# A tile of its own for the larger part of batch 0's queries

## The chip, the cores and the metric

The kernel runs on one core of a Trainium2 chip. The metric is the device time of one execution in microseconds. TensorE (PE) multiplies matrices, VectorE (DVE), ScalarE (ACT) and GpSimd (POOL) do the rest, and SyncE (SP) stores the output. Loads and stores are DMAs, which an engine issues and which then run by themselves.

## The reference

Two layers, one behind the other, on 8 batches of 576 tokens. The first is an attention with a compressed memory of 32 rows per head, the second a channel mixing.

```python
# attention: q, k, v (8, 8, 576, 64), phi (8, 8, 576, 32)
a = softmax(phi, axis=memory)
k_m, v_m = a^T k, a^T v                       # (batch, head, 32, 64)
x = softmax(q k_m^T / sqrt(64)) v_m           # heads side by side: (8, 576, 512)
# mixing: w_k (512, 1024), w_v (1024, 512), w_r (512, 512)
x_prev = x shifted by one token, zero in front
xk, xr = mu_k x + (1 - mu_k) x_prev, mu_r x + (1 - mu_r) x_prev
out = sigmoid(xr w_r) * (relu(xk w_k) ** 2 w_v)
```

All inputs and the output are float32; the kernel computes in bf16 between them.

## The kernel before

A token's number in its batch is 9 p + j, with p from 0 to 63 on the partitions (two heads fill 128) and j from 0 to 8 along the row. The tiles of one batch therefore have 128 rows, four groups of heads and nine tokens each. `qs` are two query tiles, one for even and one for odd batches, `kvs` and `ems` the same for keys with values and for the exponentials of phi.

Nothing is ordered by a scheduler. `PLAN` is a list of words that stand in the order in which the steps are written to the engines. `0:qu` is step `qu` of batch 0, `c0:0b` is a block of the product with w_k, `g:` and `o:` are blocks of the products with w_r and w_v, and `p:` is a load. Each engine takes its own steps in this order. A step that needs another engine's result waits for it, and everything behind it on that engine waits too. These waits are put in when the program is built, from what the steps read and write in which tile.

Most loads are issued by GpSimd, since they turn float32 into bf16 on the way. So its queue is a list of loads: a load that waits holds up all later ones. The words in `PRE` come first, then those of the plan:

```python
PRE = "q:0u id:"
# p:v:0g p:v:0h p:q:0t p:wk:0-4 p:wk:4-8 p:phi:1 p:k:1 p:q:1 p:wr:0-4 p:wv:0-2 p:v:1 p:wv:2-4 ...
PARTS = (slice(0, 3), slice(3, NJ))
```

Batch 0 is split finer than the others. Its phi and its keys are loaded by ScalarE's queue as float32 (`ph`, `k0f`) and cast by ScalarE and VectorE. Its queries come in two parts by j: `q:0u` loads j 3 to 8 and `q:0t` loads j 0 to 2, both into `qs[0]` (line 186). `turn_part` (line 375) transposes one part for the scores: word `0:qu` the larger part, word `0:qt` the smaller one. In the plan `0:qu` stands ahead of `p:q:0t`. The other batches' queries go through `turn_q` (line 367).

In the names of the profile, `kvps` is the product of the exponentials with keys or values (line 285), `scps` the scores (line 392 for the parts, line 413 for whole batches), `pk`, `pr` and `pv` the products with w_k, w_r and w_v (lines 636, 669, 686), and `idle` are filler matmuls on zeros (line 225) with which the plan fills stretches in which TensorE has nothing to do. `rl` and `sq` are the relu and its square (lines 644 and 651), `x` the attention's output (line 477), `qT` the transposed queries.

The pool `work` has a ring of three places under the tag `x`. Batch 0's two halves of `k0f` take the first two; the attention outputs `x` of batches 1 to 7 follow.

Of the kernel before, what the change touches and what calls it, by code (L numbers as in the profile page):

```python
# [11 lines left out]
BF16 = mybir.dt.bfloat16  # L12
# [58 lines left out]
NJ = 9  # L71
# [5 lines left out]
def kernel(  # L77
# [13 lines left out]
    nc = tc.nc  # L91
    B, H, S, D = q.shape
# [12 lines left out]
    PARTS = (slice(0, 3), slice(3, NJ))  # L105
# [7 lines left out]
    work = ctx.enter_context(tc.sbuf_pool(name="work", bufs=2))  # L113
# [8 lines left out]
    HH = H // 2  # L122
    ROWS = (slice(0, 64), slice(64, 128))
    kvs = [const.tile([128, 2, HH, NJ, D], BF16, name=f"kv{i}") for i in range(2)]
    qs = [const.tile([128, HH * NJ, D], BF16, name=f"q{i}") for i in range(2)]
# [7 lines left out]
    def rows(src):  # L133
        return src.rearrange("h s d -> (h s) d").rearrange("(a p j) d -> p a (j d)", a=HH, j=NJ)

    def load_phi(b, eng):
        ph = ld.tile([128, HH, NJ, M], F32, name="ph", tag="ph")
        eng.dma_start(out=ph.rearrange("p h j m -> p h (j m)"), in_=rows(phi[b]))  # L138
        loads[b] = ph

    def load_rows(dst, src):
        nc.gpsimd.dma_start(out=dst.rearrange("p h j d -> p h (j d)"), in_=rows(src))  # L142

    def load_parity(dst, src, r):
        nc.gpsimd.dma_start(out=dst[r].rearrange("p h j d -> p h (j d)"), in_=rows(src)[r])
# [3 lines left out]
    for gs in (slice(0, 2), slice(2, 4)):  # L149
        k0.append(work.tile([128, 2, NJ, D], F32, name="k0f", tag="x", bufs=3))  # L150
        nc.scalar.dma_start(out=k0[-1].rearrange("p h j d -> p h (j d)"), in_=rows(k[0])[:, gs])
    nc.vector.memset(zeros, 0.0)  # L152
    mu2 = const.tile([2 * ND, 128], F32, name="mu2")
    nc.sync.dma_start(out=mu2[:ND, :], in_=moe_mu_k.rearrange("(a b) -> a b", b=128))
# [12 lines left out]
    def preload(word):  # L167

        what, _, part = word.partition(":")
        if what in weights:  # L170
            dst, src = weights[what]
            f0, f1 = (int(x) * 128 for x in part.split("-"))
            nc.gpsimd.dma_start(out=dst[:, :, f0:f1], in_=src[:, :, f0:f1])  # L173
        elif what == "id":
            make_identity(nc, identity)
        else:
            n = int(part[0])
            if what == "phi":
                load_phi(n, nc.gpsimd)
            else:  # L180
                dst = qs[n % 2].rearrange("p (h j) d -> p h j d", j=NJ) if what == "q" else kvs[n % 2][:, "kv".index(what)]
                src = {"q": q, "k": k, "v": v}[what][n]
                if part[1:] in ("t", "u"):
                    js = PARTS["tu".index(part[1])]
                    cols = slice(js.start * D, js.stop * D)
                    nc.gpsimd.dma_start(out=dst[:, :, js].rearrange("p h j d -> p h (j d)"), in_=rows(src)[:, :, cols])
                elif part[1:] in ("g", "h"):
                    gs = slice(0, 2) if part[1] == "g" else slice(2, 4)
                    nc.gpsimd.dma_start(out=dst[:, gs].rearrange("p h j d -> p h (j d)"), in_=rows(src)[:, gs])
                elif part[1:]:  # L190
                    load_parity(dst, src, ROWS["ab".index(part[1])])
                else:
                    load_rows(dst, src)

    for word in PRE.split():
        preload(word)
# [50 lines left out]
    def attention(b):  # L247
# [112 lines left out]
        def q_tile():  # L360
            if "qT" not in st:
                st["qT"] = work.tile([128, HH, NJ * PB, 2], BF16, name="qT", tag="qT", bufs=2)
            return st["qT"]
# [9 lines left out]
        def turn_part(js):  # L373

            def go():
                dst = q_tile()[:, :, js.start * PB:js.stop * PB].rearrange("p g n h -> p g (n h)")
                src = qs[b % 2].rearrange("p (g j) d -> p g (j d)", j=NJ)[:, :, js.start * D:js.stop * D]
                nc.vector.transpose(dst.bitcast(U32), src.bitcast(U32))
            return go

# [326 lines left out]
    for n, word in enumerate(" ".join(PLAN).split()):  # L707
        who, _, name = word.partition(":")
        if who == "p":
            todo.append((n, -2, word, lambda name=name: preload(name)))  # L710
        elif who in mixes:
            todo.append((n, -1, word, mixes[who][name]))
        else:
            todo.append((n, int(who), word, attend[int(who)](name)))
# [36 lines left out]
```

## Time and profile before

| | us |
|---|---|
| median of 3 runs | 204.7 |
| lowest and highest of these | 204.52, 205.77 |
| the profiled execution | 205.92 |
| its span, first to last instruction | 204.1 |
| VectorE busy in it | 150.8 |
| ScalarE busy in it | 136.7 |
| mean clock granted to TensorE | 0.988 of full |

A row of the timeline has the start in us, the length in us, the engine, the line, the operation, the tiles (out <- in) and how many instructions were merged. In brackets stands the idle time of the engine just before, and what ended it. `DMA q<-in_q_dram` there means that the wait ended when that load landed, `issue` that the profile shows no cause. The largest groups of loads by issue, with the KB of one and the median time from issue to landing:

```profile
ph<-in_phi_dram POOLq DMA_DIRECT2D x7, 576.0 KB, 15.0
kv<-in_k_dram POOLq DMA_DIRECT2D x7, 576.0 KB, 15.8
q<-in_q_dram POOLq DMA_DIRECT2D x7, 576.0 KB, 18.6
kv<-in_v_dram POOLq DMA_DIRECT2D x7, 576.0 KB, 19.0
```

KB are those of the destination in bf16 for keys, values and queries; the source has twice as many.

### The profile page before, as it was taken

Reading aid. Unit: us, or ns where it says so; the run is one execution under the profiler, and the core shown is the slowest. Engines: PE = TensorE matmul, PEld = TensorE weight load, DVE = VectorE, ACT = ScalarE, POOL = GpSimd, SP = SyncE. Lnnn points to the kernel's source line nnn. Section 1 sums busy time; section 2 is a strip of 40 time slices with the busy share of each in tenths; the row PEclk is TensorE's granted clock in tenths of the full one; section 3 lists DMA queues with packets and bytes.
Section 4 is the critical chain, followed back from the end, with each engine's and each line's share of the span. In section 5 each row is a group of like instructions: output and inputs, shape, how many; then the busy total and the mean of one; then the engine's idle time right before and its main releaser. Section 6 shows DMA issues by size and latency. Waiting matters only on the chain.

```text
span 204.1 us, 5433 instructions
## 1 busy us (share of the span) xinstructions
PE 194.3 (95%) x2228; PEld 101.4 (50%) x2228; DVE 150.8 (74%) x318; ACT 136.7 (67%) x310; POOL 28.7 (14%) x43
## 2 busy tenths in 40 slices
PE   8898999999998999999998999999999999999992
PEld 8453665674444444544445864444444444444441
DVE  2266678798998998999996997999999655320351
ACT  2538699767869999899858697894638940646220
POOL 5077222211004400082000000000000000000000
PEclk9999999999999999999998899999999999999998
DMA  6999999999999999899999240042330133310085
GB/s 203 270 139 236 235 204 206 261 226 227 287 230 291 209 241 260 176 151 200 320 252 236 37 94 12 3 102 52 75 85 0 27 84 88 71 43 0 20 248 143
DMA packets 25033, 31.88 MB, mean 156 GB/s; under 512 B 2472, under 2 KB 19632, under 8 KB 25008
## 3 DMA queue, kind: packets, MB, share of 16 engines
q0 software_dynamic: 17360, 20.32, 53.5%
q1 hardware_dynamic: 6176, 8.92, 17.1%
q10 hardware_dynamic: 1472, 2.29, 3.3%
q8 instruction: 17, 0.28, 0.5%
q14 instruction: 8, 0.07, 0.1%
HBM read 38.28 MB, written 9.44 MB: 234 GB/s over the span
## 4 chain that ended last, share of the span: by engine, by line
PE 70%; DMA 19%; POOL 3%; ACT 3%; issue 1%; DVE 1%; DVEq 0%; POOLq 0%
PE pv L686 27%; PE pk L636 24%; PE pr L669 13%; DMA wr<-in_moe_w_r_dram 8%; DMA ph<-in_phi_dram 7%; DMA q<-in_q_dram 4%; PE kvps L285 3%; ACT x L477 2%; PE nops L342 1%; ACT em L261 1%; POOL kv L142 1%; PE scps L413 1%; POOL wk L173 1%; POOL ph L138 1%; PE zps L295 1%
## 5 line engine op out<-in xcount | busy, mean ns | idle before, releaser
L636 PE MATMUL pk<-xkT,wk 128*128 128x512 bf16 (+4 forms) x352 | 68.3, 342 | 0.0
L686 PE MATMUL pv<-wv,sq 128*128 128x512 bf16 (+3 forms) x328 | 66.7, 353 | 0.0
L644 ACT ACTIVATE rl<-pk 128x512 bf16<-128x512 f32 (+3 forms) x66 | 35.5, 556 | 22.5 <-PE pk L636 21.2
L636 PEld LDWEIGHTS <-wk 128*128 128x128 bf16 x352 | 33.1, 99 | 27.9 <-issue 1.8
L686 PEld LDWEIGHTS <-sq 128*128 128x128 bf16 x328 | 30.9, 98 | 29.3 <-issue 0.2
L692 DVE SCALAR_TENSOR_TENSOR o<-sg,pv 128x512 f32<-128x512 f32 (+3 forms) x41 | 24.4, 613 | 20.7 <-PE pv L686 16.8
L669 PE MATMUL pr<-wr,xrT 128*128 128x512 bf16 x144 | 35.1, 380 | 0.2 <-DMA wr<-in_moe_w_r_dram 0.2
L651 ACT ACTIVATE sq<-rl 128x512 bf16<-128x512 bf16 (+5 forms) x59 | 27.0, 494 | 0.9
L673 ACT ACTIVATE sg<-pr 128x512 f32<-128x512 f32 x36 | 20.7, 604 | 8.9 <-DVE o L692 6.2
L669 PEld LDWEIGHTS <-xrT 128*128 128x128 bf16 x144 | 13.6, 98 | 16.5 <-DMA wr<-in_moe_w_r_dram 0.4
L477 ACT CAST x<-nops 128x320 bf16<-128x320 f32 (+1 forms) x50 | 16.3, 417 | 7.6 <-PE nops L342 7.6
L653 DVE TENSOR_TENSOR sq<-rl 128x512 bf16<-128x512 bf16 (+5 forms) x45 | 14.2, 338 | 5.7 <-ACT rl L644 5.1
L502 DVE TENSOR_SCALAR mu_d<-diff,mu 128x576 bf16<-128x576 bf16 x42 | 13.8, 377 | 0.3
L225 PE MATMUL idle<-zeros 128*128 128x64 bf16 (+2 forms) x107 | 11.3, 275 | 2.0 <-DVE zeros L152 1.0
L261 ACT ACTIVATE em<-ph 128x1152 bf16<-128x1152 f32 (+1 forms) x9 | 9.4, 1063 | 5.7 <-DMA ph<-in_phi_dram 5.7
L463 DVE TENSOR_TENSOR atn<-e,lz 128x576 bf16<-128x576 bf16 (+2 forms) x18 | 11.7, 686 | 0.2
L489 DVE TENSOR_TENSOR diff<-x 128x1280 bf16<-128x1280 bf16 (+2 forms) x21 | 10.4, 552 | 1.1 <-ACT x L477 0.9
L370 DVE STREAM_TRANSPOSE qT<-q 128x576 uint32<-128x576 uint32 x14 | 10.4, 760 | 0.8 <-DMA q<-in_q_dram 0.7
L642 DVE TENSOR_SCALAR rl<-pk 128x512 bf16<-128x512 f32 (+3 forms) x14 | 8.4, 603 | 3.3 <-PE pk L636 2.5
L504 DVE TENSOR_TENSOR xkT<-x,mu_d 128x1152 bf16<-128x1152 bf16 x14 | 10.5, 754 | 0.3
L504 DVE TENSOR_TENSOR xrT<-x,mu_d 128x1152 bf16<-128x1152 bf16 x14 | 10.3, 750 | 0.1
L500 ACT ACTIVATE mu_d<-diff,mu 128x576 bf16<-128x576 bf16 x14 | 10.1, 794 | 0.4 <-DVE diff L490 0.4
(72 smaller groups left out, 154.8 us busy)
## 6 DMA issues: line engine op xcount, KB each, us to landing
out_dram<-o SPq DMA_DIRECT2D x59, 128.0 KB, 2.4
ph<-in_phi_dram POOLq DMA_DIRECT2D x7, 576.0 KB, 15.0
kv<-in_k_dram POOLq DMA_DIRECT2D x7, 576.0 KB, 15.8
q<-in_q_dram POOLq DMA_DIRECT2D x7, 576.0 KB, 18.6
kv<-in_v_dram POOLq DMA_DIRECT2D x7, 576.0 KB, 19.0
k0f<-in_k_dram ACTq DMA_DIRECT2D x2, 576.0 KB, 6.6
wk<-in_moe_w_k_dram POOLq DMA_DIRECT2D x2, 512.0 KB, 7.5
wv<-in_moe_w_v_dram POOLq DMA_DIRECT2D x2, 512.0 KB, 18.5
```

The costliest lines, as they stand in the source:

```text
L463: nc.vector.tensor_mul(st["at"][:, c, sl], st["e"][:, c, sl], st["lz"][:, c, sl])
L477: (nc.vector.tensor_copy if both and i > 1 else nc.scalar.copy)(st["x"][:, i, sl], pss[i])
L502: nc.vector.tensor_scalar_mul(t[:, i], st["d"][:, pr + i, :], mu1[:, o:o + 1])
L504: nc.vector.tensor_add(dst, st["x"][:, pr:pr + n], t)
L636: nc.tensor.matmul(pk[:, p0 - lo:p1 - lo], lhsT=wk_sb[:, di, fi * 128:(fi + 1) * 128], rhs=xk_T[:, di, p0 % RING:p0 % RING + p1 - p0], sta ...
L644: nc.scalar.activation(rl, pk, AF.Relu, scale=HALF ** 0.5)
L651: nc.scalar.activation(sq[:, fi, p:p + p1 - p0], rl[:, part], AF.Square)
L653: nc.vector.tensor_mul(sq[:, fi, p:p + p1 - p0], rl[:, part], rl[:, part])
L669: nc.tensor.matmul(pr, lhsT=xr_T[:, di, c0:c0 + 128], rhs=wr_sb[:, di, :], start=(di == 0), stop=(di == ND - 1))
L673: nc.scalar.activation(gated[t], pr, AF.Tanh, scale=0.5)
L686: nc.tensor.matmul(pv[:, cols], lhsT=sq[:, fi, p:p + 128], rhs=wv_sb[:, fi, cols], start=(fi == 0), stop=(fi == NF - 1))
L692: nc.vector.scalar_tensor_tensor(o[:, cols], in0=gated[t][:, cols], scalar=1.0, in1=pv[:, cols], op0=AL.add, op1=AL.mult)
```

## The change

The larger part of batch 0's queries gets a tile `q0u` of its own, of 128 rows x 4 groups x 6 tokens x 64 in bf16, which takes the third place of the ring under the tag `x`. The smaller part stays where it was in `qs[0]`. `q0` is the pair of both places; the load and `turn_part` take their place from it. The plan, `PRE` and the banks stay as they were, and so does the order of the instructions on every engine. In the built program GpSimd's load `q:0t` has lost its wait for VectorE; twelve loads later, the load of batch 2's keys names VectorE (besides ScalarE) among those whose reading of batch 0's keys it waits for.

```diff
+    js = PARTS[1]
+    q0 = (qs[0].rearrange("p (h j) d -> p h j d", j=NJ)[:, :, PARTS[0]],
+          work.tile([128, HH, js.stop - js.start, D], BF16, name="q0u", tag="x", bufs=3))
     nc.vector.memset(zeros, 0.0)
...
                 if part[1:] in ("t", "u"):
                     js = PARTS["tu".index(part[1])]
                     cols = slice(js.start * D, js.stop * D)
-                    nc.gpsimd.dma_start(out=dst[:, :, js].rearrange("p h j d -> p h (j d)"), in_=rows(src)[:, :, cols])
+                    dst = q0["tu".index(part[1])]
+                    nc.gpsimd.dma_start(out=dst.rearrange("p h j d -> p h (j d)"), in_=rows(src)[:, :, cols])
...
             def go():
                 dst = q_tile()[:, :, js.start * PB:js.stop * PB].rearrange("p g n h -> p g (n h)")
-                src = qs[b % 2].rearrange("p (g j) d -> p g (j d)", j=NJ)[:, :, js.start * D:js.stop * D]
+                src = q0[PARTS.index(js)].rearrange("p g j d -> p g (j d)")
                 nc.vector.transpose(dst.bitcast(U32), src.bitcast(U32))
```

## The prediction

> **What bounds the kernel now.** I read the page first, then the chain of waits, then the waits of TensorE and of the load queue, then the early stretch microsecond by microsecond.
>
> ```profile
> span 204.1 us, 5433 instructions
> ...
> PE 194.3 (95%) x2228; PEld 101.4 (50%) x2228; DVE 150.8 (74%) x318; ACT 136.7 (67%) x310; POOL 28.7 (14%) x43
> ...
> DMA  6999999999999999899999240042330133310085
> ```
>
> TensorE is busy for 194.3 of 204.1 us, so everything that can be gained by waiting less is in the other 9.8 us. The transfers run nearly full until about 112 us (slices of 5.1 us; a 9 is 90% or more). The chain of waits has the queue that the change touches at its start:
>
> ```profile
> 1.25 8.87 DMA q<-in_q_dram
> 10.12 0.02 issue
> 10.14 0.99 DVE qT L378
> 11.13 0.29 issue
> 11.42 0.76 POOL q L186
> ...
> 15.84 15.41 DMA wr<-in_moe_w_r_dram
> ```
>
> The larger part of the queries lands at 10.12, VectorE transposes it until 11.13, and only then GpSimd issues the smaller part and, behind it, every later load. The chain reaches TensorE when wr lands at 31.25. What those 30 us are worth is not their length but what TensorE waited for meanwhile. This is the view of waits between 19 and 60 us (in total, times, longest):
>
> ```profile
> PE idle L225 <- issue: 1.0, 1, 1.0
> PE scps L413 <- DVE qT L370: 0.4, 1, 0.4
> PE nops L342 <- DVE o L692: 0.2, 1, 0.2
> PE pr L669 <- DMA wr<-in_moe_w_r_dram: 0.2, 1, 0.2
> PE kvps L285 <- DMA kv<-in_k_dram: 0.2, 1, 0.2
> ```
>
> Loads end the last two directly, and the 0.4 through the transpose of batch 1's queries. The other two have other releasers.
>
> **Part 1, the wait that goes.** The queue's timeline:
>
> ```profile
> 2.63 1.43 POOL L189 DMA_DIRECT2D kv<-in_v_dram  x2
> 11.42 0.76 POOL L186 DMA_DIRECT2D q<-in_q_dram  x1 [7.36 <-DVE qT L378]
> 12.17 1.49 POOL L173 DMA_DIRECT2D wk<-in_moe_w_k_dram  x2
> 13.63 0.78 POOL L138 DMA_DIRECT2D ph<-in_phi_dram  x1
> 14.38 0.78 POOL L142 DMA_DIRECT2D kv<-in_k_dram  x1
> ```
>
> The smaller part is written into columns that the transpose doesn't read, but into the same tile, and so the built program made the load wait for the transpose: 7.36 us. With two tiles that wait is not in the built program any more. GpSimd then goes on at 4.06: 0.76 for the smaller part, 1.49 for the two of wk, 0.78 and 0.78 for phi and k of batch 1, until 7.9. The next, q of batch 1, waits in both built programs for the landing eight loads earlier, here the larger query part at 10.12. No instruction is added on any engine, and the new tile takes the third place of a three-place ring whose next user, x of batch 3, comes tens of us later. Cost 0; if that place were still held the wait would be seen on ScalarE's x casts.
>
> **Part 2, what the transfers gain.** Engine shares and GB/s by stretch (the last two numbers):
>
> ```profile
> 10.00:11.00 1.00, 1.00 (x7) 0.39 (x4) 0.86 (x1) 0.06 (x1) 0.00 (x0) 1.00 1.22 213
> 11.00:12.00 1.00, 1.00 (x41) 0.73 (x40) 0.37 (x2) 0.00 (x0) 0.58 (x1) 1.00 0.96 159
> 12.00:13.00 1.00, 0.90 (x41) 0.57 (x40) 0.62 (x4) 0.00 (x0) 1.00 (x3) 1.00 0.33 35
> 13.00:14.00 1.00, 1.00 (x52) 0.36 (x44) 0.69 (x3) 0.39 (x2) 1.00 (x2) 1.00 0.99 89
> 14.00:15.00 1.00, 1.00 (x40) 0.59 (x40) 0.48 (x1) 0.90 (x4) 1.00 (x2) 1.00 1.44 190
> ```
>
> GpSimd waits 7.36 us, but the transfers starve for much less, because what it had issued lasts until nearly 12. Against 213 the four stretches from 11 to 15 miss 54 + 178 + 124 + 23 = 379 KB, or 379 / 213 = 1.8 us. I take 1.8 for every landing behind it. The bounds are 0.8 (only the empty stretch 12 to 13 counts, 178 / 213) and 2.0 (a little for 15 to 16 beside). The loads ahead of the gap (larger query part, v, k) stand first in their queues as before: 0 for them, and VectorE has 0.63 us of idle behind the first transpose to cover a later landing:
>
> ```profile
> 11.75 0.61 DVE L323 TENSOR_SCALAR kbd<-kvps,rz 128x128 bf16<-128x128 f32 x2 [0.63 <-PE kvps L285]
> ...
> 15.13 0.58 DVE L378 STREAM_TRANSPOSE qT<-q 128x384 uint32<-128x384 uint32 x1 [0.16 <-DMA q<-in_q_dram]
> ```
>
> The second row is the smaller part's own transpose. It waited 0.16 us for its load; that goes, and is worth 0, because TensorE's wait at 18.82 (part 4) stands between it and the end.
>
> **Part 3, what TensorE gains.** The three waits in their places:
>
> ```profile
> 24.17 0.37 PE L295 MATMUL zps<-ones,em 128*128 128x2 bf16 x9
> ...
> 24.39 1.03 PE L636 MATMUL pk<-xkT,wk 128*128 128x256 bf16 x8
> ...
> 25.59 0.75 PE L285 MATMUL kvps<-kv,em 64*32 64x64 bf16 x72 [0.16 <-DMA kv<-in_k_dram]
> ...
> 27.38 0.44 ACT L644 ACTIVATE rl<-pk 128x320 bf16<-128x320 f32 x1 [0.35 <-PE pk L636]
> ...
> 28.44 0.78 DVE L370 STREAM_TRANSPOSE qT<-q 128x576 uint32<-128x576 uint32 x1 [0.70 <-DMA q<-in_q_dram]
> ...
> 30.13 0.45 PE L413 MATMUL scps<-qT,kmT 32*32 32x288 bf16 x24 [0.35 <-DVE qT L370]
> ...
> 31.30 3.63 PE L669 MATMUL pr<-wr,xrT 128*128 128x512 bf16 x16 [0.17 <-DMA wr<-in_moe_w_r_dram]
> ...
> 33.73 1.08 ACT L651 ACTIVATE sq<-rl 128x320 bf16<-128x320 bf16 x3
> ```
>
> k lands 1.8 earlier than 25.59: 0.16 goes. q of batch 1 lands near 26.6 instead of 28.4, VectorE's 0.70 of idle goes, so the transposes end some 0.7 earlier, and the 0.35 goes. wr lands near 29.4 and is wanted near 30.3: 0.17 goes. Together 0.68. A gap is counted from the modelled end of the matmul before it, and without a wait the next group starts inside that end (zps ends at 24.54, pk starts at 24.39, an overlap of 0.15), so each of the three is worth about 0.1 more: 1.0. Landings only 0.8 earlier would still do for the first and, nearly, for the last.
>
> Against this stands ScalarE. At 27.38 it waits for TensorE, which by then has won only 0.25; from there to the squares that end at 34.81 its rows follow each other without a pause. So the squares come 0.25 earlier: the first of the three near 33.85 (a third of 1.08 behind 33.73, less 0.25), the last at 34.56. The value matmuls that read them stand behind the pr group, which would end at 34.93 - 1.0 = 33.93. If the first square decides, nothing is lost; if the last, 0.6. I take 0.1, near the first, because the last one's reader comes later within the group. Won: 0.9, bounds 0.3 and 1.1.
>
> **To the end.** Later loads wait for TensorE, and TensorE once more for ScalarE:
>
> ```profile
> 49.01 0.74 POOL L142 DMA_DIRECT2D kv<-in_v_dram  x1 [6.04 <-PE kvps L285]
> ...
> 62.67 0.92 PE L285 MATMUL kvps<-kv,em 64*32 64x128 bf16 x72 [0.94 <-ACT x L477]
> ...
> 87.05 0.74 POOL L142 DMA_DIRECT2D kv<-in_k_dram  x1 [18.60 <-PE kvps L285]
> ```
>
> The loads of 49.01 and 87.05 start when kvps has read the buffer that they fill, so they move with TensorE, and what the transfers had won beyond TensorE's 0.9 is given back as idle transfers ahead of them. The 0.94 us at 62.67 waits for casts of what TensorE itself made just before, so it moves along unshortened. Nothing in the chain of waits after 110 us names a load, so the 0.9 reaches the end.
>
> **Part 4, the wait that stays, and a rule.** The longest wait is at no load's place:
>
> ```profile
> 18.82 0.27 PE L225 MATMUL idle<-zeros 128*128 128x256 bf16 x1 [0.98 <-issue]
> ...
> q8 instruction: 17, 0.28, 0.5%
> ```
>
> It is a filler that waits for no semaphore. The 17 packets of the instruction queue hold 0.28 MB, which over TensorE's 2 x 2228 instructions is 63 bytes each, 16 KB or some 260 instructions a packet. I read the 0.98 us as TensorE waiting for that block. The change leaves the place where the block is asked for, so 0 is taken, with a bound of 1.0 won and 2 lost.
>
> [...]
>
> **The sum.** 204.1 - 0.9 = 203.2 us of span. The profiled execution took 205.92 us, 1.8 more than its span, and the median of the runs is 204.7, so by the same 0.9 I predict 203.8.
>
> **Rivals.**
> - *The block of instructions comes later* (slower). Between 12 and 14 us the transfers had room, 35 and 89 GB/s, and a block is asked for some us before it is used. With the gap filled it queues behind loads. It decides from 0.9 us of delay; with 2 us TensorE starts again at 20.8, and the time is 204.7 - 0.9 + 2 = 205.8. Against it: most blocks of the first 110 us were asked for under full transfers, and no second wait of this kind stands in the list. 13%. [...]
> - *The 0.98 us is wk's.*
>
> ```profile
> DMA to landing us min/median/max: 6.6/7.5/8.4
> ```
>
> This is of wk's two halves: the first, issued at 12.17, landed about 18.8, just when the filler started. Then 0.9 more goes, 204.7 - 1.8 = 202.9. Against it: the filler doesn't read wk, and at 25.59 and 31.30 only the reader itself waited. 9%.
> - *Nothing arrives at the end.* ScalarE and VectorE pace the stretch from 22 to 38, TensorE's three waits turn into waits for casts, or the landings win only 0.8: 204.4 to 204.8. For it: ScalarE's rows without a pause from 27.38 to 34.81. 18%.
> - Something not seen here: 4%, half of it on each side.
>
> **Numbers.** The forecast, 203.3 to 204.4, has 56%. The range of 202.7 to 205.2 takes in wk's rival, the rival of no effect and the smaller half of the fetch rival. About 1% (2.05 us: below 202.65, above 206.75) is what a measurement tells from no change. Faster by more: part of wk's rival with the upper bounds, and the unseen, 9%. Slower by more: a fetch that is over 3 us late, and the unseen, 7%. Within: 84%.
>
> **What would show it.** The smaller part is issued near 4.1 with no wait; 12 to 14 us move some 200 GB/s; wr lands near 29.4; the three waits at 25.6, 30.1 and 31.3 are gone; the filler still waits about 1 us near 18.8; pr starts near 30.3. I am wrong if the filler's wait grows by more than it wins, if landings behind 15 us are not 1 us earlier, or if TensorE wins the three waits and loses them before 60 us.

## The result, and the profile after

| | before | after |
|---|---|---|
| median, 20 runs of each on one chip | 204.84 us | 203.35 us |
| lowest and highest | 203.41, 206.58 | 201.88, 205.05 |
| ratio, 95% interval | 1 | 0.9932 [0.9905, 0.9959] |
| the profiled execution (span) | 205.92 (204.1) | 202.75 (201.0) |

The kernel is 0.7% faster, 1.5 us by the medians; 203.8 was predicted, with a range of 202.7 to 205.2. The two profiled executions lie 3.2 us apart, twice as much. The runs spread over 3 us, and part of that goes with TensorE's clock (of the kernel after, the 15 runs with a mean granted clock of 0.995 or more have a median of 203.14 us, the other five 204.85): some executions of either kernel have a stretch at half the clock, and that, with a late wait ahead of it, is why one profile differs from the next by more than the medians do.

The page of the kernel after, its span, TensorE's busy time and the transfers (40 slices of 5.0 us):

```profile
span 201.0 us, 5434 instructions
...
PE 192.8 (96%) x2228; PEld 100.8 (50%) x2228; DVE 150.5 (75%) x318; ACT 136.3 (68%) x310; POOL 28.9 (14%) x43
...
DMA  6999999999999999899999240042420233210185
```

The work is the same. TensorE's 1.5 us less of busy time are for the most part the stretch at half the clock that the profile before has, 0.50 for 3.4 us from 110.6 on, and this one hasn't (below). Now the load queue's timeline, and engine shares and GB/s by stretch (GB/s is the last number):

```profile
4.06 0.77 POOL L190 DMA_DIRECT2D q<-in_q_dram  x1
4.81 1.50 POOL L176 DMA_DIRECT2D wk<-in_moe_w_k_dram  x2
...
10.04 0.74 POOL L142 DMA_DIRECT2D q<-in_q_dram  x1 [2.13 <-DMA q0u<-in_q_dram]
12.53 0.74 POOL L176 DMA_DIRECT2D wr<-in_moe_w_r_dram  x1 [1.75 <-DMA kv<-in_v_dram]
```
```profile
12.00:13.00 1.00, 0.98 (x70) 0.71 (x70) 0.66 (x3) 0.00 (x0) 0.47 (x1) 1.00 1.49 191
13.00:14.00 1.00, 1.00 (x55) 0.52 (x40) 0.29 (x1) 0.79 (x4) 0.69 (x2) 1.00 1.30 206
```

The smaller part is issued at 4.06 instead of 11.42, and the stretch from 12 to 13 moves 191 GB/s instead of 35. By the group of wr's load (16.9 us from issue to landing) wr lands at 12.53 + 16.9 = 29.4, where it landed at 31.25. What TensorE makes of it, in its timeline:

```profile
18.54 0.27 PE L229 MATMUL idle<-zeros 128*128 128x256 bf16 x1 [1.10 <-issue]
...
25.08 0.75 PE L289 MATMUL kvps<-kv,em 64*32 64x64 bf16 x72
...
28.85 0.49 PE L417 MATMUL scps<-qT,kmT 32*32 32x288 bf16 x32
29.39 0.60 PE L640 MATMUL pk<-xkT,wk 128*128 128x256 bf16 x4
29.82 3.62 PE L673 MATMUL pr<-wr,xrT 128*128 128x512 bf16 x16
```

The three waits are gone, the filler's is still there, and pr starts at 29.82 instead of 31.30. For comparison two rows of before that stand around its wait for qT:

```profile
29.45 0.32 PE L413 MATMUL scps<-qT,kmT 32*32 32x288 bf16 x8
...
30.52 0.61 PE L636 MATMUL pk<-xkT,wk 128*128 128x256 bf16 x4
```

From there TensorE stays 1.5 us ahead until 103 us. Of these 1.48 us 0.28 are already there at the filler, and they look like chance: TensorE's first sums (`zps`) start at 6.17 instead of 6.59 here, and in the twelve other profiles below anywhere from 6.33 to 6.69, with no order between kernels with the change and without it. The other 1.20 come behind the filler. From 103 us on the lead grows again, to 3.2 us from 113 us on. The chain of waits shows the place, in the kernel before and then in the kernel after (start, length, what):

```profile
90.34 15.03 DMA ph<-in_phi_dram
105.40 2.22 ACT em L261 x2
```
```profile
88.81 14.59 DMA ph<-in_phi_dram
103.42 2.22 ACT em L265 x2
```

Both kernels wait late for phi of batches 6 and 7. What follows on TensorE in the kernel before, with its clock (the third number from the right) by stretch:

```profile
107.98 0.36 PE L295 MATMUL zps<-ones,em 128*128 128x2 bf16 x9 [0.64 <-ACT x L477]
```
```profile
108.00:110.00 2.00, 1.64 (x19) 0.89 (x19) 1.03 (x3) 1.62 (x5) 0.00 (x0) 1.00 1.21 208
110.00:112.00 2.00, 2.00 (x101) 1.63 (x105) 0.99 (x3) 1.49 (x5) 0.00 (x0) 0.65 1.17 253
112.00:114.00 2.00, 2.00 (x86) 1.65 (x66) 1.93 (x6) 1.04 (x4) 0.00 (x0) 0.50 0.65 125
```

TensorE idles 0.64 us, and soon after it runs at half its clock. In the profile after the wait at this place is 0.17 and the clock stays at 1.00. Nothing of the change lies there. That made two questions: how much of the gain belongs to the change, and what the late wait does to it.

### The profile page after: what moved, and what is told of

The parts are those of the page before. It is cut to its first block, busy times and chain, and to the rows that moved or that the text cites. A ratio compares the mean times of both kernels' runs of the same rounds, so it can differ in the third digit from the quotient of the medians.

```text
span 201.0 us, 5434 instructions
## 1 busy us (share of the span) xinstructions
PE 192.8 (96%) x2228; PEld 100.8 (50%) x2228; DVE 150.5 (75%) x318; ACT 136.3 (68%) x310; POOL 28.9 (14%) x43
## 4 chain that ended last, share of the span: by engine, by line
PE 80%; DMA 9%; ACT 5%; issue 2%; DVE 1%; POOL 1%; DVEq 0%
PE pk L640 27%; PE pv L690 27%; PE pr L673 13%; DMA ph<-in_phi_dram 9%; PE kvps L289 4%; PE idle L229 3%; ACT em L265 2%; ACT x L481 2%; PE nops L346 1%; PE scps L417 1%; PE mxps L346 1%; PE zps L299 1%; POOL kv L142 1%; DVE kbd L327 1%; ACT rl L648 1%
## 5 line engine op out<-in xcount | busy, mean ns | idle before, releaser
L690 PEld LDWEIGHTS <-sq 128*128 128x128 bf16 x328 | 30.9, 98 | 29.4 <-issue 0.2
L696 DVE SCALAR_TENSOR_TENSOR o<-sg,pv 128x512 f32<-128x512 f32 (+3 forms) x41 | 24.4, 614 | 19.8 <-PE pv L690 15.8
L506 DVE TENSOR_SCALAR mu_d<-diff,mu 128x576 bf16<-128x576 bf16 x42 | 13.8, 377 | 0.3
## 6 DMA issues: line engine op xcount, KB each, us to landing
ph<-in_phi_dram POOLq DMA_DIRECT2D x7, 576.0 KB, 14.9
```

The source lines that it names most:

```text
L506: nc.vector.tensor_scalar_mul(t[:, i], st["d"][:, pr + i, :], mu1[:, o:o + 1])
L690: nc.tensor.matmul(pv[:, cols], lhsT=sq[:, fi, p:p + 128], rhs=wv_sb[:, fi, cols], start=(fi == 0), stop=(fi == NF - 1))
L696: nc.vector.scalar_tensor_tensor(o[:, cols], in0=gated[t][:, cols], scalar=1.0, in1=pv[:, cols], op0=AL.add, op1=AL.mult)
```

## The experiments

Twelve kernels, in three sets; each set has runs of the kernel before on its chip. "Full clock" below means a run whose mean granted clock is 0.995 or more.

**The two kernels once more.** n0_before is the kernel before, n1_after the kernel after, both unchanged.

> The kernel before, unchanged, to see how much its traces and clocks differ among themselves. Theory (the wait): ratio 1.00, and its runs are granted about the same clocks as those of the changed kernel, 0.988 to 1.0. Rival (the clock): its runs are granted 0.988 clearly more often than those of the changed kernel, and runs of equal clock differ by less than 0.5 us between the two kernels. In the trace: TensorE's first sums (zps) start near 6.6 us if the 0.4 us at the start belongs to the change, anywhere from 6.1 to 6.7 if it is chance.

> The changed kernel, unchanged, as the measure for the others of this call: ratio 0.993 to the kernel before, 203.4 us. Its trace shows whether the 1.1 us of the filler near 18.5 us stand in every execution: theory (with the transfers full the block of instructions is always late) a wait of 0.8 to 1.3 us there again; rival (chance, as in the kernel before, of whose two traces one has none) none.

Measured: n0_before 204.77, ratio 0.9998 [0.996, 1.0037]. n1_after 204.04 with 204.26 beside it, ratio 1.0019 [0.9978, 1.006]: no gain that can be told, against 0.9932 on the first occasion. In n1_after 6 of 12 runs lacked the full clock, on the first occasion 5 of 20; the kernel before lacked it in 3 of 12, and beside the sets in 6 of 23, 7 of 28 and 5 of 11, so it doesn't lose the clock more often. The runs of the kernel after with the full clock agree, 203.37 and 203.14. Those of the kernel before don't, 204.63 in the first set and 203.95 in the second, so that by full clocks n1_after is 0.6 us faster. In the two profiles the kernel after is 1.7 us ahead from 38 to 105 us and 0.6 at the end. The profile of n1_after shows the late wait again, now 1.17 us, and the half clock behind it:

```profile
107.37 0.36 PE L299 MATMUL zps<-ones,em 128*128 128x2 bf16 x9 [1.17 <-ACT x L481]
```
```profile
106.00:108.00 2.00, 0.80 (x11) 0.50 (x11) 1.91 (x5) 2.00 (x5) 0.00 (x0) 1.00 1.20 230
108.00:110.00 2.00, 1.78 (x9) 0.64 (x9) 0.00 (x0) 1.49 (x5) 0.00 (x0) 0.57 1.19 220
110.00:112.00 2.00, 2.00 (x76) 1.40 (x77) 0.65 (x2) 1.11 (x3) 0.00 (x0) 0.50 1.12 238
```

So the late wait and the clock belong to neither kernel. The profile of n0_before tells something on the filler, too: it doesn't wait at 18 us there, but TensorE stops a little later for phi of batch 1:

```profile
24.87 0.38 PE L295 MATMUL zps<-ones,em 128*128 128x2 bf16 x9 [1.24 <-ACT em L261]
```

Before the change two causes stand one behind the other in this stretch, and in these profiles either costs about 1 us if the other doesn't (0.98 in the profile of before, 1.24 here).

**The wait put back, and made longer.** e1_wait_back is the kernel after, with a copy of two elements of the transposed larger part on GpSimd ahead of the smaller part's load. Nobody reads the copy. e2_wait_longer copies from a later tile.

```diff
-    ... 0:l1 0:l1 p:q:0t ...
+    ... 0:l1 0:l1 0:hold p:q:0t ...
+        def hold():
+            held = work.tile([128, 2], BF16, name="held", tag="held", bufs=1)
+            nc.gpsimd.tensor_copy(held, st["qT"][:, 0, 3 * PB, :])    # e2: st["kmT"][:, 0, 0:2]
```

> The changed kernel with its two tiles, but GpSimd first copies two elements of the transposed larger part, so the wait is back and the tiles stay. Theory (the wait): the load of the smaller part is issued near 11.5 us, the transfers starve between 12 and 14 us, TensorE's three waits for k, q and wr are back, and the time is that of before, 204.8. Rival (the tile's place, not the wait): it keeps what the changed kernel won, 203.4.

> As the one with the wait put back, but the copy reads the transposed keys, which VectorE has ready some 1.4 us later, near 12.7 us. Theory (landings decide TensorE's waits one for one): all loads land 1.4 us later than in the kernel before, the waits for k, q and wr grow by 1.4 us between them, 206.2 us. Rival (casts on ScalarE and VectorE pace this stretch and hide landings): under 0.5 us more than before, 205.3 at most.

Measured: e1 205.85, ratio 1.005 [1.0014, 1.0086]; its five runs with the full clock have a median of 204.84, the 17 such runs of before beside it 204.63. e2 208.19, ratio 1.0131 [1.0078, 1.0184]. The load is issued at 11.42 in e1 (38 GB/s from 12 to 13 us) and at 13.26 in e2:

```profile
13.13 0.18 POOL L387 COPY held<-kmT 128x2 bf16<-128x2 bf16 x1 [9.06 <-DVE kmT L361]
13.26 0.76 POOL L190 DMA_DIRECT2D q<-in_q_dram  x1
```
```profile
13.00:14.00 1.00, 0.99 (x54) 0.33 (x38) 0.72 (x3) 0.35 (x2) 0.87 (x2) 1.00 0.09 19
14.00:15.00 1.00, 1.00 (x40) 0.63 (x40) 0.48 (x1) 0.91 (x4) 1.00 (x3) 1.00 0.29 13
```

The wait alone takes the gain away: in e1 the queries have their own tile and nothing is won. (This set has no run of the kernel after; the gain is that of the other occasions.) The three waits that the expectation names don't come back as such, though: the filler, k and wr have no wait in e1's profile, and TensorE waits 0.92 us for phi of batch 1 at 24.53 instead, then 0.41 for wv and 0.52 for values by 63 us. And the wait has a price by length: 1.84 us more of it cost 2.3 us more by the medians, but part of that is the clock. Five of e2's six runs lacked the full clock, and the one that had it took 206.03, 1.2 us more than e1's five. That is near the 206.2 expected, and not by the waits expected: in e2 TensorE waits 2.09 us from 15.88 on for the smaller part and 1.05 for phi, while those for k and q are 0.18 and 0.36, as in the kernel before, and wr has none.

**The other way to fill the gap.** e6_wk_first leaves the tile and the wait of the kernel before, and moves the first half of wk ahead of the smaller part.

```diff
-    ... 0:l1 0:l1 p:q:0t ... 0:st p:wk:0-4 0:l0 ...
+    ... 0:l1 0:l1 p:wk:0-4 p:q:0t ... 0:st 0:l0 ...
```

> The kernel before, with one query tile, and the first half of wk loaded ahead of the smaller query part: GpSimd still waits for the transpose, but the transfers have wk to move meanwhile. Theory (what cost time is that the transfers starve): 12 to 13 us move over 150 GB/s, loads from phi of batch 1 on land over 1 us earlier, and 1.0 to 1.5 us are won, 203.4 to 203.9; the smaller part lands up to 1.5 us later, near 16, at the cost of up to 0.5 of it. Rival (the smaller part must come earlier): 204.8 or slower.

Measured: 204.71, ratio 1.0007 [0.9966, 1.0049]. The stretch from 12 to 13 us moves 203 GB/s, but the smaller part lands late:

```profile
17.94 0.39 PE L392 MATMUL scps<-qT,kmT 32*32 32x96 bf16 x32 [2.03 <-DVE qT L378]
```
```profile
16.00:18.00 2.00, 0.06 (x16) 0.06 (x16) 0.69 (x2) 0.47 (x2) 2.00 (x3) 0.92 1.19 209
18.00:20.00 2.00, 2.00 (x46) 0.75 (x50) 1.19 (x3) 0.68 (x4) 0.47 (x1) 0.50 1.12 327
```

The room is filled and nothing is won: the wait costs 2 us, and the clock falls to 0.50 behind it. 11 of 12 runs lacked the full clock. The other took 202.98, 1.0 us less than the runs of before with the full clock beside it (203.95), so filling the gap may be worth something that the late part takes back; one run doesn't show it. As it stands, filling the gap wasn't enough, because the smaller part lost its place for it.

**The block of instructions.** The 17 packets of the instruction queue hold 0.28 MB in the profile of before, 16 KB each. If they are cut by count, an edit that leaves instructions out ahead of the filler moves the place at which a block is needed. e3_fetch40 is the kernel after with 40 of TensorE's instructions fewer in the first fillers (20 of the 78 left out, 20 made twice as wide), e4_fetch78 the same with 78 fewer, e5_before_fetch40 the edit of e3 in the kernel before.

```diff
-    keep_busy(*WARM)
+    ps = ps_tile([128, CT], F32, "idle")
+    for n in [1] * 38 + [2] * 20:    # e4: [2] * 39
+        nc.tensor.matmul(ps[:, :n * 64]..., lhsT=zeros, rhs=zeros[:, :64]..., start=True, stop=True, ...)
```

> The changed kernel with 20 of the first 78 fillers made twice as wide and 20 left out: the same filler work in 40 instructions less on TensorE, so that every 256th instruction is another one. Theory (the wait near 18.5 us is for a block of instructions): that wait is gone and no other comes, TensorE is held next by casts near 18.1, 0.3 to 0.6 us won, 202.9 us. Rival (it is for wk, which lands near 17 us now, or for anything else at that place): the filler still waits 1.0 to 1.1 us and the time stays 203.4.

> The changed kernel with 39 fillers of double width in place of 78: 78 instructions less, so that the borders between blocks of 256 instructions lie 78 places later in the rest of the program. Theory (blocks of 256, each asked for when the one before is entered): the filler near 18.5 has no wait, but one without a releaser of 0.4 to 1.2 us appears near 25.5 us inside the mxps group behind batch 1's kvps, whose block is entered only some 4.5 us earlier; 202.6 to 203.4 us. Rival (any cut of instructions ahead helps, or none does): 202.3 as with 40 less, with no new wait, or 203.4 with the filler's wait as it was.

> The kernel before with the same 40 instructions less. Theory (without the change the loads decide: where the block comes in time, TensorE waits near 24 us for phi of batch 1 instead): 0 to 0.4 us won against the kernel before, 204.4 to 204.8, with a wait of zps for em near 24.5. Rival (both gains are independent and add): 1.1 won, 203.7.

Measured: e3 202.31, ratio 0.9873 [0.9832, 0.9913]; e4 206.71, 1.0121 [1.005, 1.0192]; e5 203.65, 0.9988 [0.9955, 1.0021]. In e3 and e5 the filler waits no more, and in e4 two other places do, of which the first is where the count puts it:

```profile
26.04 0.41 PE L350 MATMUL mxps<-atn,vmm 32*64 32x256 bf16 x19 [0.76 <-issue]
...
111.72 0.41 PE L293 MATMUL kvps<-kv,em 64*32 64x128 bf16 x30 [2.41 <-issue]
```

The wait goes where the count of instructions goes: it is the block. With two instructions a matmul, the filler that waits is number 700 of TensorE in the profiles of before, after, n1_after and e7 (below); in e4 the two waits stand at 956 and 3254, which is 256 and nearly ten times 256 further. And in all six places a packet of the instruction queue starts 2.2 to 2.4 us ahead of the wait's end (at 16.40 for 18.82 in the profile of before, at 16.22 for 18.54 in the profile after). e4 is slower than the 202.6 to 203.4 expected: its second wait wasn't expected, and four of its six runs lacked the full clock (the other two: 204.56 and 204.69). e5 wins 0.3 us by full clocks, 203.64 against 203.95, with waits for wk (0.50), phi (0.24) and wr (0.57).

The time of e3 seemed to show that the block is worth 1 us at the end. But at 100 us TensorE in e3 is 0.7 us later than in the profile after, 0.5 of it from the first sums on (6.68 against 6.17): what it had won at 18 us was gone by 51, 0.6 of it in waits that the view puts down to loads of keys. Its gain comes at 106, because phi of batches 6 and 7 landed earlier on this occasion (ScalarE waits 0.6 us for it, in the profile after 1.9). The number spoke for the block and the trace doesn't; the next set decides.

**The late wait taken away.** The loads of phi for batches 6 and 7 move ahead of the load of batch 7's keys, so that they no longer stand behind loads that wait for TensorE at 86 us. e8_before_phi is this in the kernel before, e7_after_phi in the kernel after; e10_before_phi_fetch40 and e9_after_phi_fetch40 have the 40 instructions fewer beside.

```diff
-    "c3:0s p:k:7 3:r0e ... o:9 c3:7s p:phi:6 c3:1s ... o:13 p:phi:7 g:14 p:k:6 ..."
+    "c3:0s p:phi:6 p:phi:7 p:k:7 3:r0e ... o:9 c3:7s c3:1s ... o:13 g:14 p:k:6 ..."
```

> The kernel before with the loads of phi for batches 6 and 7 issued directly ahead of batch 7's k (about 68 and 82 us instead of behind the loads of 85 to 90 us). Theory (ScalarE's late wait for these two makes TensorE idle 0.2 to 1.4 us near 107 us, and after an idle of 0.6 us or more the granted clock falls to 0.5 for some microseconds): ScalarE's wait of 2 to 3 us for phi near 105 us is gone, TensorE has no gap over 0.3 us between 104 and 110 us, the granted clock is 0.995 or more in most of the runs, and the time is 203.2 to 203.8 us where the kernel before takes 204.7 beside it. Rival (the clock falls for a cause of its own): as many runs with a clock under 0.995 as of the kernel before, and 204.5 us.

> The same move in the kernel after. Theory (the change's own gain is made before 35 us and is independent of the wait near 105 us): 0.9 to 1.2 us below the kernel before with the same move, about 202.4 us. Rival (the change gained only by drawing fewer runs with a low clock): equal to the kernel before with the same move within 0.3 us.

> The kernel after with the move of phi and 40 fillers fewer at 18 us (20 left out, 20 doubled). Theory (three causes that are independent: the token part's wait, the wait for the block of instructions, the late wait for phi): 0.4 to 1.0 us below the kernel after with the move of phi alone, 201.0 to 201.8 us. Rival (the block's wait is hidden by another wait behind it): equal to the kernel after with the move alone within 0.3 us.

> The kernel before with the move of phi and 40 fillers fewer. Theory (in the kernel before the late transfers hold TensorE at the same place when the block's wait is gone): 0 to 0.4 us below the kernel before with the move alone. Rival (the block's wait counts there as it does in the kernel after): 0.8 to 1.1 us below it.

| six runs of each | us | lowest, highest | ratio to before, 95% interval |
|---|---|---|---|
| e8: before, phi moved | 202.67 | 202.50, 203.13 | 0.9884 [0.9853, 0.9914] |
| e7: after, phi moved | 201.44 | 201.32, 201.62 | 0.9821 [0.9791, 0.985] |
| e10: before, phi moved, 40 fewer | 203.15 | 202.90, 203.43 | 0.9903 [0.9873, 0.9933] |
| e9: after, phi moved, 40 fewer | 201.37 | 201.18, 201.65 | 0.9821 [0.9788, 0.9853] |

The kernel before took 205.19 beside them, from 204.00 to 207.35. All 24 runs of the four have the full clock, and each kernel's spread is 0.3 to 0.6 us instead of 3. Three things follow.

First, the change by itself: 202.67 - 201.44 = 1.23 us, and the ranges don't touch. In the two traces TensorE's lead is 1.38 us when pr starts, 1.22 from 62 us on, and 1.22 still at 171 us. The rival of that pair, that the gain had only been a matter of the clock, is out. The waits that differ are others than in the first pair of profiles. These are rows of e8, then of e7:

```profile
24.48 0.38 PE L295 MATMUL zps<-ones,em 128*128 128x2 bf16 x9 [1.32 <-ACT em L261]
...
31.48 0.82 PE L669 MATMUL pr<-wr,xrT 128*128 128x512 bf16 x3 [0.45 <-DVE rl L642]
```
```profile
18.82 0.27 PE L229 MATMUL idle<-zeros 128*128 128x256 bf16 x1 [0.90 <-issue]
...
30.10 2.11 PE L673 MATMUL pr<-wr,xrT 128*128 128x512 bf16 x9
```

In e8 the filler doesn't wait, TensorE is 1.4 us ahead of e7 behind it, 0.37 of that from the start, and then loses the lead to phi's 1.32 us and to waits at scps and pr. In e7 the block costs 0.90, and those three waits are gone.

Second, the late wait: it was worth more than expected, 2.2 us against the six runs of before with the full clock (204.85), and that without any loss of clock. The wait that the view names is only a part of it, as the same stretch of the kernel after shows, here as it is and then in e7:

```profile
106.00 0.36 PE L299 MATMUL zps<-ones,em 128*128 128x2 bf16 x9 [0.17 <-ACT x L481]
106.33 0.92 PE L346 MATMUL nops<-atn,vb 32*64 32x256 bf16 x3
107.48 0.30 PE L346 MATMUL nops<-atn,vb 32*64 32x256 bf16 x5 [0.23 <-ACT sg L677]
107.72 1.04 PE L673 MATMUL pr<-wr,xrT 128*128 128x512 bf16 x4
```
```profile
105.72 0.37 PE L299 MATMUL zps<-ones,em 128*128 128x2 bf16 x9
106.02 0.32 PE L346 MATMUL nops<-atn,vb 32*64 32x256 bf16 x8
106.27 1.04 PE L673 MATMUL pr<-wr,xrT 128*128 128x512 bf16 x4
```

Two waits of 0.40 us together are read, and pr starts 1.45 us later. The rest hides in the row of three matmuls that take 0.92 us: ScalarE, late itself, empties the sums late (its casts of x start at 105.54, in e7 at 103.54).

Third, the block of instructions. e9 is no faster than e7, so the rival is right there: TensorE is 0.21 us ahead of e7 at 15 us, 1.06 at 19, 0.62 at 25, 0.39 at 41, 0.07 at 62. It is given away in small pieces, one of them at a load of keys. These are the waits of TensorE in e9 from 17 to 62 us:

```profile
PE kvps L293 <- ACT x L485: 1.0, 1, 1.0
PE nops L350 <- DVE o L700: 0.2, 1, 0.2
PE kvps L293 <- DMA kv<-in_k_dram: 0.2, 1, 0.2
PE ktps L359 <- DVE kbd L331: 0.2, 1, 0.2
```

In e10 the edit even costs 0.5 us: with the block out of the way TensorE is held by loads at four places, wk's (0.5 us, at 18.89) first. Both expectations of e10, a gain in either case, were wrong.

The fastest kernel of all is e7, with e9 beside it: 201.4 us, 1.8% below the kernel before.

## Why the prediction was right

- **The wait that goes, and the transfers** (parts 1 and 2): as written. Issue at 4.06 for "near 4.1", some 200 GB/s from 12 to 14 us, wr at 29.4 for "near 29.4". The next load waits for the larger part, as the built program had told.
- **TensorE's three waits** (part 3): right in mechanism, and the term was mis-sized: 0.9 was taken, bounds 0.3 and 1.1, and 1.20 was measured in the first pair of profiles, behind the 0.28 of the start. The runs of e7 against e8 give 1.23 too, but there the sum is made of other waits (phi's and the block's, above), so the terms are borne out by the first pair alone. From start to start, before against after: the kvps step 0.23 (0.26 taken), from scps to the next pk 1.07 - 0.54 = 0.53 (0.45 taken), from that pk to pr 0.78 - 0.43 = 0.35 (0.27 taken), and 0.09 in between. The overlap was put at 0.1 a wait and is nearer to 0.2 where the wait cut a group in two. The 0.1 that ScalarE was to take back wasn't taken: its e row starts at 30.01 instead of 30.63 and its squares at 33.10 instead of 33.73, 0.63 us of which 0.28 are the start's, so it won 0.35 where 0.25 was reckoned, and pv followed pr without a wait. Nor are the 9.8 us of idle time all that waiting can cost: at 106 us 0.40 us of idle time stood for 1.45.
- **The filler's wait at 18.82, priced at 0** (part 4): right in sum, and by luck. That it is the block is shown by e3 and e4, so wk was not its cause; yet wk stood half hidden behind it, since in e5, with the block gone, TensorE waits 0.5 us for wk. Against the profile of before, the first rival, a block later by 0.9 or more, didn't come: 1.10, 1.0 and 0.90 us in the profiles after, n1_after and e7 against 0.98. What that profile couldn't show is that the wait is not always there: in n0_before and e8 it is absent, and phi's 1.24 and 1.32 us stand in its place. Against these two the rival did come: the block's packet starts at 15.31 and 14.85 us there and at 16.22 to 16.59 with the change, and the filler's wait is new; that the packet queues behind loads, as the rival has it, no run shows. The 0 held because phi's wait, which the sum didn't have either, went and was about as long.
- **To the end**: this is the step that failed. "Nothing in the chain of waits after 110 us names a load, so the 0.9 reaches the end" is true as a sentence, and the chain named phi's load from 90.34 to 105.37, just ahead of that mark, with ScalarE waiting for it. The gain reaches the end all the same, because phi is issued behind loads that wait for TensorE's kvps (87.05 before, 85.52 after), and so it moved with TensorE. But the time from issue to landing of these two loads varied, from 12.3 and 13.3 us in e3 to 14.7 and 15.6 in n0_before and n1_after and 14.9 and 15.8 in e2, and with it ScalarE's wait for them (0.6 us in e3, 3.1 in e2) and the clock behind it (1.00 and 0.50). That is as large as the change. It fits that 1.5 us were measured on one occasion and nothing on another; e7 and e8 show what the change brings when the late wait is out of the way. Why phi lands earlier or later was not tried.

The rival of no effect had ScalarE's rows without a pause for it; they moved as a whole. The measured 203.35 lies 0.45 below the forecast: 0.3 from the mis-sized term, and the rest within what two occasions differ by.

## What to carry to other kernels

In this program a write into one part of a tile was ordered behind a read of another part, on a queue that issues most of the loads. The wait cost less than its length, and less than what the transfers missed: it was 7.36 us of waiting, 1.8 of transfers by the prediction's estimate from their GB/s, and 1.2 at the end. A wait is best sized from start to start against the same step without it, since the idle time in a row left out what overlap and slow neighbours hid (0.40 us of it stood for 1.45 at 106 us). And a chain of waits is to be read to its last load, wherever that stands: here a transfer that ended a wait late in the kernel went with a spread of 3 us, larger than the change's 1.2, and with the loads of phi moved the spread was 0.3 to 0.6. It pays to take such a wait away first and to measure the change then.

## What the runs showed of the hardware

- TensorE's clock fell to 0.50 for 3 to 7 us behind idle times of 0.64 us (before), 1.17 (n1_after), 1.23 (n0_before), 1.36 (e2, at 111 us) and 2.03 (e6). It did not behind 2.09 us at the same place as e6's (e2), 1.32 at 24 us (e8), 0.98 at 18 (before) and 2.41, the longest, at 112 (e4). So an idle time of 0.6 us or more doesn't suffice, though e8's expectation says so, and two of nearly one length at one place (2.03 us in e6, 2.09 in e2) ended differently. What decides it was not shown.
- TensorE stood still for its own instructions: 0.76 to 2.41 us in the rows with no releaser, at a place that moves with the count of instructions (e3, e4). The packet for the block at 18 us starts at 13.8 us in e2, where the transfers idle (13 to 15 us: 19 and 13 GB/s), at 14.9 to 15.3 in e8, e1 and n0_before, and at 16.2 to 16.6 in after, n1_after and e7, with the gap filled. But the profile of before has the gap as well (35 GB/s from 12 to 13 us) and its packet at 16.4, so what moves the packet isn't shown. What such a wait was worth was settled by the waits behind it: e7 has 0.90 us of it and e9 none, and at 62 us e9 is 0.07 ahead.
